# First-softmax maxima moved from one VectorE reduction to a ScalarE copy, GpSimd folds and a short VectorE minimum, with a new table of slots

## The chip, the core and the metric

The kernel runs on one core of a Trainium2 chip. The core has five engines that run their own instruction queues in order and wait for each other through semaphores: TensorE (PE; its weight loads are shown as PEld), VectorE (DVE), ScalarE (ACT), GpSimd (POOL) and SyncE (SP, which here only starts DMA transfers). SBUF is the on-chip memory of 128 partitions, PSUM the eight banks that PE writes. The metric is the device time of one execution in microseconds (us). Three runs of the kernel before took 719.73 to 719.92 us, median 719.89.

## The reference

```
def _attn_ref(x, inducing):            # x: 4 x 12416 x 128, inducing: 32 x 128
    scale = 1.0 / np.sqrt(C)
    I = np.broadcast_to(inducing[None], (B, m, C))
    def mab(q, kv):
        s = scale * (q @ kv.transpose(0, 2, 1))
        s = s - s.max(-1, keepdims=True)
        a = np.exp(s)
        a /= a.sum(-1, keepdims=True) + 1e-09
        return a @ kv
    h = mab(I, x)
    return mab(x, h)

def _moe_ref(x, w_gate, w_val, w_out): # x: 49664 x 128, d_ff 1536
    gate = 1.0 / (1.0 + np.exp(-(x @ w_gate)))
    val = x @ w_val
    return gate * val @ w_out
```

The 32 inducing rows attend over each batch's 12416 tokens (the first softmax, over tokens), each token then attends over the 32 results `h` (the second softmax, over 32), and a gated feed-forward layer follows.

## The kernel before

**Tiling.** A batch's 12416 tokens lie as 97 columns of 128 tokens, cut into six groups of 16 columns and a single column (group index 6). The feed-forward layer works on blocks of four columns (512 tokens): 24 blocks a batch and one last block made of the four single columns, 97 in all. The hidden width of 1536 is 12 chunks of 128. The weights are multiplied with `h` once a batch (`hw`), so that a chunk of a block needs a matmul with only 32 rows.

**Steps and slots.** Chunks are taken two and one at a time; a step has two chunks or one, a slot is a pair of steps, so three chunks. In a step `product` (L964) writes the value matmuls `v`, then the gate matmuls of two steps later (`gate_fill`), then DVE's product `u = (t + 1) * v` (L981), where `t = tanh(g/2)` comes from ACT (`gate`, L962). At the end of each odd step `project` (L1050) takes up to 12 or 16 output matmuls of 128 columns (L1062) from a queue; a finished block is scaled by ACT into `o` (L1081) and sent out by SP. A batch lasts 96 slots, and `base[b]` is its first.

**Work beside the steps.** Everything else is put into slots by hand. `at(slot, make, late)` keeps a list; `beside` calls what stands there: plain entries behind the even step of the slot, late ones behind the odd step, those with `side` inside `product`. An entry's instructions go to their engines' queues at that place.

- First softmax of batch b+1, during batch b (`plan_stage1`, L332): in slot `score` PE writes scores of one group into a PSUM bank (`s1_score_pe`, L255) and DVE takes the negated maximum over 512 columns (`s1_max`, L267); one slot later ACT takes the exponential with that maximum as bias (`s1_exp`, L280); in the next SP transposes the result by DMA (L304); later PE sums (`s1_sum_pe`) and ACT keeps the sums (L330). The groups have maxima of their own; `plan_combine` joins them.
- Second softmax (`plan_stage2`, L617): PE scores (L483), ACT copies to SBUF (`s2_take`, L520), POOL finds the maximum of 32 by five levels of subtract, clip at 0 and add (`s2_lower_pool`, L530 to L535), ACT takes the exponential (L544), POOL sums, inverts and spreads (L552 to L598), SP transposes into `a2r` (L609), from which the gate and value matmuls read.
- Asides (`plan_aside`, L1007): nine chunks of batch 3 are left out of the steps; ACT and POOL make their product instead of DVE.
- Loads of `x` for batch b+2 (b+1 in batch 0) are DMA transfers started by POOL (L96); SP transposes them into `xT` (L105).

**Banks.** PSUM has one bank each for `g1`, `v1`, `m` and `acc` and two each for `g2` and `v2`. All beside work takes turns on `m`.

Batch 0's own first softmax is in the prologue (`PROLOGUE`, the functions beginning with `p_`), ahead of the first product at 30.5 us.

Of the kernel before, what the change touches and what calls it, by code (L numbers as in the profile page):

```python
# [37 lines left out]
def kernel(  # L38
# [179 lines left out]

    summed = [0] * B
    def keep_on(n, tag):  # L220
# [11 lines left out]
    def at(slot, make, late=False, side=False):  # L232
        plan.setdefault((slot, "side" if side else late), []).append(make)
# [15 lines left out]
    def s1_score_pe(b, s, tag, s1=None):  # L249
        c0, n = groups[s]  # L250
        ng, w, R = s1_dims(s)
        if s1 is None:
            s1 = ps.tile([P, 512], F32, tag=tag, name="s1_ps")
# [35 lines left out]
    def s1_turn_pe(b, s, a1T, tag="m"):  # L289
        ng, w, R = s1_dims(s)  # L290
        aT = ps.tile([P, 4, P], F16, tag=tag, name="aT_ps")
# [15 lines left out]
    def s1_sum_pe(b, s, a1, hp, k0, k1):  # L307
        c0, n = groups[s]
# [23 lines left out]
    def plan_stage1(b, s, score, total):  # L332
# [15 lines left out]
        at(score, begin)  # L348
        at(score + 1, weigh, late=full)
        at(score + 2, turn)  # L350
        first, second, keep = total

        def part(k0, k1):
            if k0 == 0:
                st["hp"] = ps.tile([P, C + 1], F32, tag="m", name="hp_ps")
# [4 lines left out]
        at(keep, lambda: s1_sum_keep(b, s, st["hp"]))  # L360
# [21 lines left out]
    def hw_fill(b, hf, tag):  # L382
        hw_ps = ps.tile([P, NI // 2, P], F32, tag=tag, name="hw_ps")
# [32 lines left out]
    def plan_combine(b, lead, weights, fill):  # L416
# [36 lines left out]
        def total():  # L453
            lh = ps.tile([P, 2, m], F32, tag="m", name="lh_ps")
# [4 lines left out]
        def part(hf):  # L459
            st["hw_ps"] = hw_fill(b, hf, "m")  # L460

        def keep(hf):
            if hf == 0:
                st["hwt"] = bp.tile([P, NI, P], F16, tag="hw", bufs=B, name="hwt")
            nc.scalar.copy(out=st["hwt"][:, ts(hf, NI // 2), :], in_=st["hw_ps"][:])
            if hf == 1:
# [724 lines left out]
```

## Time and profile before

| | us |
|---|---|
| median of three runs | 719.89 |
| span of the profiled execution, first to last instruction | 718.4 |
| first product starts | 30.51 |
| last product ends | 714.0 |
| products on DVE (771) | 670.9 |
| tanh on ACT (770) | 589.5 |

The profiled execution's own time is its span plus what lies around it; the runs' median is 1.5 us above the span. In a row of groups stand line, engine, operation, what is written and read with its shape, the count, then the busy time in us and the mean of one instruction in ns, then the idle time of the engine just before them and what ended most of it. Rows of one engine can overlap by some tens of ns, since the next instruction begins before the last is written out; the busy time counts such a stretch once. In a timeline row stand start, duration, engine, line and count of merged neighbours. The queues have names with q (SPq, DVEq).

### The profile page before, as it was taken

The page shows a single profiled execution, that of the slowest core. Times are in us where ns is not written, and L with a number is a line of the kernel's source. Part 1 is how long each engine was busy: PE and PEld are TensorE (multiplying, and loading weights), DVE is VectorE, ACT ScalarE, POOL GpSimd, SP SyncE. Part 2 cuts the span into 40 slices and gives each one's busy share as a digit, 9 for nine tenths or more (in the row PEclk, how much of TensorE's full clock was granted, in tenths as well). Part 3 has the DMA queues.
Part 4 walks back from the last instruction along what each step waited for, and adds up shares of the span by engine and source line. Part 5 has one row for each costly group of instructions (what it writes and reads, how often), then busy time and mean ns, then how long its engine had stood idle before and what let it go on. Part 6 is the DMA issues. An engine that isn't in the chain of part 4 may idle for free.

```text
span 718.4 us, 21566 instructions
## 1 busy us (share of the span) xinstructions
PE 650.5 (91%) x8446; PEld 394.2 (55%) x8446; DVE 702.4 (98%) x872; ACT 675.1 (94%) x1019; POOL 445.8 (62%) x718
## 2 busy tenths in 40 slices
PE   8889889999998998999989988999899999999897
PEld 4455555555555555555555555555555555555555
DVE  5899999999999999999999999999999999999997
ACT  4699999999999999999999999999999999999996
POOL 4574763888653747588666266387766787676220
PEclk9999999999999999999999999999999999999999
DMA  9796696244568344335268431220222122223011
GB/s 209 115 182 130 125 165 105 75 90 106 89 133 162 80 103 92 59 79 119 66 117 161 102 75 51 70 74 31 77 60 73 46 62 67 39 75 71 35 46 46
DMA packets 118182, 65.77 MB, mean 92 GB/s; under 512 B 101408, under 2 KB 102208, under 8 KB 118080
## 3 DMA queue, kind: packets, MB, share of 16 engines
q1 hardware_dynamic: 112176, 50.90, 31.6%
q0 software_dynamic: 5584, 13.34, 10.9%
q8 instruction: 66, 1.08, 0.6%
q14 instruction: 36, 0.29, 0.1%
q10 hardware_dynamic: 320, 0.15, 0.1%
HBM read 27.80 MB, written 25.43 MB: 74 GB/s over the span
## 4 chain that ended last, share of the span: by engine, by line
PE 51%; ACT 24%; DVE 16%; issue 5%; DMA 2%; DVEq 1%; POOL 1%; ACTq 0%
PE acc_ps L1062 24%; ACT t L962 22%; PE v_ps L944 21%; DVE u L981 14%; PE g_ps L944 2%; DMA xn<-in_x_dram 2%; PE s_ps L483 2%; PE hp_ps L315 1%; ACT o L1081 1%; DVE nm L267 1%; DVEq L981 1%; ACT a1T L280 0%; PE s_ps L255 0%; POOL xn L96 0%; ACTq L962 0%
## 5 line engine op out<-in xcount | busy, mean ns | idle before, releaser
L981 DVE SCALAR_TENSOR_TENSOR u<-t,v_ps 128x1024 f16<-128x1024 f16 (+1 forms) x771 | 670.9, 945 | 1.7 <-PE g_ps L944 0.8
L962 ACT ACTIVATE t<-g_ps 128x1024 f16<-128x1024 f32 (+1 forms) x770 | 589.5, 822 | 22.2 <-ACT t L962 10.3
L944 PE MATMUL v_ps<-a2r,hwt 32*128 32x512 f16 (+1 forms) x1179 | 290.8, 371 | 56.9 <-DVE u L981 53.2
L1062 PE MATMUL acc_ps<-wo,u 128*128 128x128 f16 x4620 | 324.5, 220 | 0.9
L1062 PEld LDWEIGHTS <-u 128*128 128x128 f16 x4620 | 259.9, 98 | 89.5 <-issue 88.1
L944 PE MATMUL g_ps<-a2r,hwt 32*128 32x512 f16 (+1 forms) x1179 | 294.0, 376 | 0.0
L944 PEld LDWEIGHTS <-hwt 32*128 32x128 f16 x2382 | 93.5, 91 | 188.6 <-issue 142.2
L552 POOL TENSOR_TENSOR sum<-e 128x256 f32<-128x256 f16 (+1 forms) x23 | 15.5, 672 | 133.8 <-ACT e L544 130.0
L598 POOL TENSOR_TENSOR a2n<-e,rs 128x2048 f16<-128x2048 f16 (+3 forms) x25 | 86.8, 3474 | 4.8 <-DVE rs L570 3.1
L576 POOL TENSOR_TENSOR near<-sme,minus 128x16 f32<-128x16 f32 (+1 forms) x22 | 65.3, 2966 | 1.8
L1081 ACT ACTIVATE o<-acc_ps 128x512 f32<-128x512 f32 x96 | 58.4, 609 | 0.0
L531 POOL TENSOR_SCALAR rise<-rise 128x256 f32<-128x256 f32 (+6 forms) x110 | 51.2, 466 | 9.7
L532 POOL TENSOR_TENSOR top<-top,rise 128x128 f32<-128x128 f32 (+3 forms) x88 | 28.4, 323 | 7.3
L552 POOL TENSOR_TENSOR sum<-sum 128x128 f32<-128x128 f32 (+3 forms) x92 | 28.4, 309 | 7.2
L530 POOL TENSOR_TENSOR rise<-top 128x128 f32<-128x128 f32 (+3 forms) x88 | 27.3, 310 | 6.9
L530 POOL TENSOR_TENSOR rise<-sc 128x256 f32<-128x256 f32 (+1 forms) x22 | 16.3, 739 | 20.9 <-ACT sc L520 20.6
L1031 POOL TENSOR_TENSOR xn_spare<-xn_spare 128x512 f16<-128x512 f32 x9 | 11.4, 1270 | 22.2 <-ACT xn_spare L1029 22.0
L535 POOL TENSOR_TENSOR sc<-sc,top 128x512 f32<-128x512 f32 (+1 forms) x22 | 23.9, 1086 | 1.7
L1026 POOL TENSOR_SCALAR xn_spare<-xn_spare 128x512 f32<-128x512 f16 x9 | 13.4, 1493 | 11.2 <-ACT xn_spare L1025 11.2
L483 PEld LDWEIGHTS <-xT 128*128 128x128 f16 x388 | 13.1, 96 | 11.7 <-issue 11.3
L280 ACT ACTIVATE a1T<-s_ps,nm 128x512 f16<-128x512 f32 (+1 forms) x26 | 16.4, 630 | 3.1 <-DVE nm L267 3.0
L483 PE MATMUL s_ps<-hT,xT 128*128 128x32 f16 x388 | 18.1, 178 | 0.1
(150 smaller groups left out, 291.4 us busy)
## 6 DMA issues: line engine op xcount, KB each, us to landing
out_dram<-o SPq DMA_DIRECT2D x96, 256.0 KB, 2.2
xn<-in_x_dram POOLq DMA_DIRECT2D x18, 512.0 KB, 7.7
xn<-in_x_dram POOLq DMA_DIRECT2D x3, 544.0 KB, 6.9
xn<-in_x_dram POOLq DMA_DIRECT2D x3, 256.0 KB, 12.8
xn<-in_x_dram SPq DMA_DIRECT2D x1, 576.0 KB, 4.8
xn<-in_x_dram SPq DMA_DIRECT2D x1, 512.0 KB, 3.9
a2r<-a2n SPq DMA_TRANSPOSE x29, 4.5
wg<-in_moe_w_gate_dram POOLq DMA_DIRECT2D x1, 384.0 KB, 12.7
```

What stands on the lines that cost most here:

```text
L483: nc.tensor.matmul(s2[:, j, :], xT[b][:, c + j, :], hT16[b][:], start=(j == 0), stop=whole and j == j1 - 1, skip_group_check=True,)
L530: nc.gpsimd.tensor_tensor(out=r, in0=far, in1=near, op=ALU.subtract)
L531: nc.gpsimd.tensor_scalar_max(out=r, in0=r, scalar1=0.0)
L532: nc.gpsimd.tensor_tensor(out=top[:, 0:n, 0:w], in0=near, in1=r, op=ALU.add)
L552: nc.gpsimd.tensor_tensor(out=d[:, 0:n, :], in0=src[:, :, 0:w], in1=src[:, :, w : 2 * w], op=ALU.add)
L576: nc.gpsimd.tensor_tensor(out=near[:, 0:n], in0=sme[:, 0:n], in1=minus1[:, 0:n], op=ALU.pow)
L598: eng.tensor_tensor(out=a2n[:, 0:n, :, :], in0=e.unsqueeze(2).to_broadcast((P, n, 4, m)), in1=rs.unsqueeze(2).unsqueeze(3).to_broadcast((P ...
L944: st[what + "end"] = nc.tensor.matmul(pt[:, k, col : col + nb * P], hw[b][r : r + 32, j // 2, :], a2r[r : r + 32, o : o + nb, :].rearrange ...
L962: st["tanh"] = nc.scalar.activation(out=st["t"][:], in_=st["g"][:], func=AF.Tanh, scale=0.5)
L981: u = nc.vector.scalar_tensor_tensor(out=st["u"][:, :, c:e], in0=st["t"][:, :, c:e], scalar=1.0, in1=st["v"][:, :, c:e], op0=ALU.add, op1= ...
L1062: nc.tensor.matmul(acc[0][(i // 2) % len(acc[0])][:, i, :], u[:, ts(i, P)], wo16[:, j, :], start=(i in fresh), stop=not any(e[2] == ib and ...
L1081: nc.scalar.mul(out=o32[:], in_=acc[0][0][:], mul=0.5)
```

## The change

Some first-softmax groups of batches 1 to 3 get another way to their maximum. In slot `score` PE writes the scores and ACT copies them, negated, to SBUF (`leave`). POOL folds the 512 columns to 64 by three levels of subtract, clip and subtract (`lower_tree`). In a later slot `done` DVE takes the minimum of the 64 (`finish`), and in slot `weight` or behind it ACT takes the exponential from the SBUF copy (`weigh_low`). A group with six slots in the table goes this way, one with four as before. The slots of nearly all beside work come from a new table, `TIMES`: its first entry serves batch 0, the second batches 1 and 2, the third batch 3. In the second some groups are scored in slots below zero, that is in the batch before, and the `xT` transposes (`turn`) stand nine slots ahead of their scores. The slots of the `x` loads are the same.

Besides: the asides leave out the last chunks of a block, and steps may hold chunks of two blocks; some aside fills and takes have another place in the step; projections of a block may run early or finish a block when 28 (in two blocks 20) or more matmuls wait; pools of `u`, `t` and `o` shrink. `BEHIND`, `DROPPED` and `SWAP` are empty and `GAP` is 0, so that the code that reads them changes nothing.

```diff
-ASIDE = {3: ((2, 9, 3, 8), (11, 17, 7, 1), (23, 26, 7, 0), (50, 53, 15, 3), (58, 62, 19, 11), (64, 69, 19, 10), (73, 76, 20, 5), (78, 81, 23, 11), (83, 88, 23, 10))}
-LATE = (4, 19, 32, 46, 43)
+ASIDE = {3: ((-1, 'm', 7, 'm', 3), (11, 'm', 17, 'm', 7), (23, 'mf', 27, 'm', 7), (50, 'm', 53, 'm', 14), (58, 'mf', 62, 'm', 19), (66, 'm', 69, 'm', 19), (73, 'm', 76, 'm', 19), (80, 'ma', 81, 'm', 23), (84, 'm', 92, 'ma', 23))}
+BEHIND = ()
+DROPPED = ()
+SWAP = ()
+GAP = 0
+BRISK = (81, 93)
+TIMES = (
+    {
+        "late": {2: (6, 7, 13, None), 3: (18, 19, 27, None), 4: (31, 33, 45, None), 5: (56, 57, 65, 52)},
+        "sum": ((10, 19, 22, 35, 35, 35), (13, 40, 41, 41), (25, 33, 37, 48, 49, 50), (37, 51, 51, 51), (42, 48, 49, 55, 55, 55), (45, 54, 54, 54), (22, 27, 27, 30)),
+        "join": (57, 61, (76, 78), (81, 83)),
+        "next": ((73, 74, 81), (86, 87, 94)),
+        "turn": (3, 7, 16, 21, 31, 37, 12),
+    },
+    {
+        "late": {2: (0, 3, 18, None), 3: (16, 21, 34, None), 4: (36, 37, 50, None), 5: (56, 57, 65, 52)},
+        "sum": ((9, 17, 17, 34, 35, 35), (13, 18, 26, 47, 48, 49), (-6, 3, 6, 50, 51, 51), (29, 35, 39, 45, 46, 46), (-3, 23, 24, 25), (31, 42, 42, 54, 55, 55), (39, 42, 43, 43)),
+        "join": (56, 60, (76, 78), (81, 83)),
+        "next": ((72, 74, 81), (86, 87, 93)),
+        "turn": (0, 4, -15, 20, -12, 22, 30),
+    },
+    {
+        "late": {2: (4, 6, 14, None), 3: (19, 21, 29, None), 4: (32, 34, 42, None), 5: (46, 48, 56, 43)},
+    },
+)
+LOW = 64
+NEGS = 4
...
-    up = ctx.enter_context(tc.tile_pool(name="up", bufs=6))
-    tp = ctx.enter_context(tc.tile_pool(name="tp", bufs=4))
-    op = ctx.enter_context(tc.tile_pool(name="op", bufs=4))
+    up = ctx.enter_context(tc.tile_pool(name="up", bufs=4))
+    tp = ctx.enter_context(tc.tile_pool(name="tp", bufs=3))
+    op = ctx.enter_context(tc.tile_pool(name="op", bufs=3))
+    sp = ctx.enter_context(tc.tile_pool(name="sp", bufs=1))
...
+    def lower_tree(low, neg):
+        w, src = 2 * P, neg
+        rise1 = s2p.tile([P, (GC + NLO) * (m // 2)], F32, tag="sum16", name="rise1")
+        top1 = s2p.tile([P, (GC + NLO) * (m // 2)], F32, tag="sum16", name="top1")
+        while w >= LOW:
+            near, far = src[:, 0:w], src[:, w : 2 * w]
+            r = rise1[:, 0:w]
+            nc.gpsimd.tensor_tensor(out=r, in0=near, in1=far, op=ALU.subtract)
+            nc.gpsimd.tensor_scalar_max(out=r, in0=r, scalar1=0.0)
+            dst = low if w == LOW else top1
+            nc.gpsimd.tensor_tensor(out=dst[:, 0:w], in0=near, in1=r, op=ALU.subtract)
+            src = dst
+            w //= 2
...
+        def leave():
+            st["neg"] = sp.tile([P, 4 * P], F32, tag="neg", name="neg", bufs=NEGS)
+            st["low"] = sp.tile([P, LOW], F32, tag="low1", name="low1", bufs=NEGS)
+            nc.scalar.mul(out=st["neg"][:], in_=st["s1"][:], mul=-1.0)
+            side_done()
+            lower_tree(st["low"], st["neg"])
+
+        def finish():
+            nm, _, col = s1_col(b, s)
+            nc.vector.tensor_reduce(
+                out=nm[:, col], in_=st["low"][:], axis=AX.X, op=ALU.min
+            )
+
+        def weigh_low():
+            nm, _, col = s1_col(b, s)
+            st["a1T"] = s1p.tile([P, 512], F16, tag="a1T", name="a1T")
+            nc.scalar.activation(
+                out=st["a1T"][:], in_=st["neg"][:], func=AF.Exp, bias=nm[:, col], scale=-1.0
+            )
+
+        if len(total) > 3:
+            done, weight, *total = total
+            at(score, fill)
+            at(score, leave, late=True)
+            at(done, finish)
+            at(weight, weigh_low, late=True)
+            at(weight + 1, turn)
+        else:
+            at(score, begin)
+            at(score + 1, weigh, late=full)
+            at(score + 2, turn)
...
     for i, n in enumerate(apart):
+        odd = (chunks[-1][1] + 1) % 2 if chunks else 0
+        js = [*range(odd, NJ), *range(odd)]
+        chunks += [(i, j) for j in js[: NJ - n]]
+        beyond.append(js[NJ - n :])
...
-            ready = waiting(t - 1)
+            room = 3 * BC - early if behind or not brisk else 3 * BC
             if acc[0] is None:
-                pace = 4 * BC if ready >= 6 * BC else 3 * BC
-            project(t - 1, t, pace)
+                brisk = waiting(t - 1) >= (5 if queue and queue[-1][2] in quick else 7) * BC
+                if brisk:
+                    room = 4 * BC
+            elif block_left() <= 4 * BC - early:
+                room = block_left()
+            project(t - 1, t, room)
```

More of the change, by code (lines that the diff above doesn't have):

```diff
@@ L217, with side_tile, side_done, side_swap @@
         )
+    side = {"acc": "acc", "m": "m", "used": 0}
+    def side_tile(shape, dtype, name):
+        side["used"] += 1
+        return ps.tile(shape, dtype, tag=side["m"], name=name)
+    def side_done():
+        side["used"] -= 1
+    def side_swap(slot):
+        if side["used"] == 0 and slot in SWAP:
+            side["acc"], side["m"] = side["m"], side["acc"]
     summed = [0] * B
+    tensor_uses = [0]
     def keep_on(n, tag):
@@ L230, with at @@
     plan = {}
-    def at(slot, make, late=False, side=False):
-        plan.setdefault((slot, "side" if side else late), []).append(make)
+    def at(slot, make, late=False):
+        slot -= sum(d <= slot for d in DROPPED)
+        plan.setdefault((slot, late), []).append(make)
     def s1_col(b, s):
@@ L968, in product @@
             keep_on(3, "acc")
-        gate_fill(t + 2)
+        if t % 2 == 0:
+            beside(t // 2, "first")
+        if t // 2 not in behind_at:
+            gate_fill(t + 2)
+            if t % 2 == 0:
+                beside(t // 2, "next")
+        elif t % 2:
+            gate_fill(t + 1)
+            gate_fill(t + 2)
         if t % 2:
@@ L1015, in fill @@
             nc.tensor.matmul(
-                st[what][:],
+                st[what][:, 0, :],
                 hw[b][r : r + 32, j // 2, :],
@@ L1084, in project @@
                 acc[0] = None
+                side_swap(now // 2)
                 if now < NST:
                     return
-    base = [first_step[(b, 0)] // 2 for b in range(B)]
     for b in range(B):
@@ L1140, in waiting, with block_left @@
         return n
-    for a in aside:
-        plan_aside(*a)
+    def block_left():
+        return sum(1 for e in queue if e[2] == queue[-1][2])
+    for b, table in ASIDE.items():
+        for n, (g, gb, v, vb, i) in enumerate(table):
+            k = sum(e[-1] == i for e in table[:n])
+            i += b * NG * GC // BC
+            plan_aside(base[b] + g, gb, base[b] + v, vb, i, beyond[i][k])
     for t in range(2):
```

178 lines of the change are left out of this document (103 added, 75 removed).

## The prediction

> **What bounds the kernel now.** I read the page first: busy times, then the costliest groups.
>
> ```profile
> span 718.4 us, 21566 instructions
> PE 650.5 (91%) x8446; PEld 394.2 (55%) x8446; DVE 702.4 (98%) x872; ACT 675.1 (94%) x1019; POOL 445.8 (62%) x718
> ...
> L981 DVE SCALAR_TENSOR_TENSOR u<-t,v_ps 128x1024 f16<-128x1024 f16 (+1 forms) x771 | 670.9, 945 | 1.7 <-PE g_ps L944 0.8 <-PE v_ps L944 0.2
> ```
>
> DVE is busy for 98% of the span, and in front of its 771 products it stood idle for 1.7 us in all. The chain of waits names PE and ACT more often, but only as the way a product's inputs came; the idle column decides. Next the four batches, from the first product to the last, by busy time:
>
> ```profile
> core 0: us, PE busy (x) PEld busy (x) DVE busy (x) ACT busy (x) POOL busy (x), PEclk, DMA share, GB/s
> 30.51:202.14 171.63, 155.31 (x2065) 94.25 (x2065) 171.35 (x207) 165.25 (x247) 114.24 (x191) 1.00 0.64 121
> 202.14:372.72 170.58, 155.25 (x2057) 94.35 (x2057) 170.54 (x205) 164.51 (x247) 110.55 (x184) 1.00 0.48 99
> 372.72:543.17 170.45, 154.84 (x2057) 94.14 (x2057) 170.45 (x204) 164.50 (x247) 107.11 (x178) 1.00 0.32 78
> 543.17:714.00 170.83, 159.33 (x1941) 97.34 (x1940) 169.46 (x196) 164.99 (x245) 100.38 (x135) 1.00 0.21 56
> ```
>
> DVE fills every batch to within 0.3 us, except the last with its tail. So whatever leaves DVE shortens the kernel, as long as nobody else comes late. The slack beside it: about 6 us a batch on ACT, 15 on PE, 57 to 70 on POOL. A slot (two steps, three chunks) lasts about 1.73 us.
>
> **Maxima on DVE: the gain.** The forms of DVE's reductions, and one in its place:
>
> ```profile
> L267 DVE TENSOR_REDUCE nm<-s_ps 128x1 f32<-128x512 f32 x22 | 15.0, 683 | 0.1
> ...
> L267 DVE TENSOR_REDUCE nm<-s_ps 32x1 f32<-32x128 f32 x4 | 1.1, 271 | 0.0
> ...
> L424 DVE TENSOR_REDUCE ml<-nm 128x1 f32<-128x7 f32 x3 | 0.5, 153 | 0.0
> ```
> ```profile
> 217.10 0.68 DVE L267 TENSOR_REDUCE nm<-s_ps 128x1 f32<-128x512 f32 x1
> 217.70 5.27 DVE L981 SCALAR_TENSOR_TENSOR u<-t,v_ps 128x512 f16<-128x512 f16 x6
> ```
>
> The 683 ns of a row overlap the next instruction by about 80 ns (217.10 to 217.70 is 0.60 us). The overlap is the same before and after, so I take differences of rows. A minimum over 64 does not occur. Between 7 elements at 153 ns and 512 at 683 ns lies 1.05 ns an element, so 64 cost 153 + 57 x 1.05 = 213 ns, and a group saves 683 - 213 = 470 ns. Bounds: 153 ns (530 saved) and the 128-element row, 271 ns (412 saved). The description says 12 groups; in the table I count those with six slots: 3 in the first entry and 5 in the second, which serves two batches, so 13. Gain: 13 x 0.470 = **6.1 us**, bounds 5.4 and 6.9; with 12 groups 5.6.
>
> [...]
>
> **ACT: copies added, hidden.**
>
> ```profile
> 209.11 1.51 ACT L962 ACTIVATE t<-g_ps 128x1024 f16<-128x1024 f32 x2 [0.22 <-ACT t L962]
> 210.51 0.60 ACT L1081 ACTIVATE o<-acc_ps 128x512 f32<-128x512 f32 x1
> 210.99 3.10 ACT L962 ACTIVATE t<-g_ps 128x1024 f16<-128x1024 f32 x4
> ```
> ```profile
> L520 ACT COPY sc<-s_ps 128x512 f32<-128x512 f32 x22 | 13.1, 595 | 0.0
> L544 ACT ACTIVATE e<-sc 128x512 f16<-128x512 f32 x18 | 11.4, 635 | 0.0
> ...
> L516 ACT ACTIVATE e<-s_ps 128x512 f16<-128x512 f32 x1 | 0.6, 603 | 0.0
> ```
>
> A scaled copy of this size holds ACT for 0.48 us (210.51 to 210.99). The exponential now reads SBUF: 635 against 603 ns, 0.03 more. A new group thus adds 0.51 us; five in a batch add 2.6 while the batch shrinks by 2.35. ACT's idle 6.1 us becomes about 1.1, in batch 0 (three groups) 3.4. That covers it only as an average. A plain slot leaves ACT 0.22 us or more, so one copy is worked off in about two slots; the table sets copies on slots other than those with a block's `o`. Cost taken: 0. Without this cover 13 x 0.51 = 6.6 us would return. The copy frees PSUM bank `m` in its own slot instead of one slot later, so no later fill waits longer for it.
>
> **POOL: folds added; who stands behind them.**
>
> ```profile
> 46.91 0.73 POOL L530 TENSOR_TENSOR rise<-sc 128x256 f32<-128x256 f32 x1
> ...
> 52.43 0.24 POOL L530 TENSOR_TENSOR rise<-top 128x32 f32<-128x32 f32 x1
> ...
> 54.46 1.08 POOL L535 TENSOR_TENSOR sc<-sc,top 128x512 f32<-128x512 f32 x1
> ```
> ```profile
> 200.84 0.67 POOL L552 TENSOR_TENSOR sum<-e 128x256 f32<-128x256 f16 x1 [5.25 <-ACT e L544]
> ...
> 207.41 3.61 POOL L598 TENSOR_TENSOR a2n<-e,rs 128x2048 f16<-128x2048 f16 x1
> ```
>
> The second softmax's fold chain takes 46.91 to 55.54 = 8.63 us; its first three levels have the shapes of the new folds: 46.91 to 52.43 = **5.52 us** a group. Its sums, inverse and spread take 200.84 to 211.02 = 10.18 us. In batches 1 and 2 five groups add 27.6 us to 107 to 111, inside 168.
>
> What matters is the queue. Behind each fold stand sums, spreads and `x` loads; behind the minimum on DVE stands every later product, and behind that PE's fills. The tightest minimum is slot 18 of batches 1 and 2. From slot 88.2 of the batch before (its chain's copy is done) the queue holds chain 8.63, folds 5.52, sums and spread 10.18, chain 8.63, folds 5.52 twice: 44.0 us or 25.3 slots, so ready at 17.5; DVE gets there at 18.65. Margin 2.0 us, cost 0. Each microsecond beyond it would be one on DVE.
>
> Does a busier POOL slow DVE? Two stretches of 8 us, POOL busy for 6.75 and for 0.00 us:
>
> ```profile
> 47.00:55.00 8.00, 6.89 (x86) 3.93 (x82) 8.00 (x11) 7.66 (x13) 6.75 (x16) 1.00 1.07 211
> 57.00:65.00 8.00, 7.25 (x101) 4.54 (x101) 8.00 (x10) 7.64 (x12) 0.00 (x0) 1.00 1.08 179
> ```
> ```profile
> L981 DVE SCALAR_TENSOR_TENSOR u<-t,v_ps 128x1024 f16<-128x1024 f16 x5 | 6.1, 1211 | 0.0
> ```
> ```profile
> L981 DVE SCALAR_TENSOR_TENSOR u<-t,v_ps 128x1024 f16<-128x1024 f16 x5 | 6.1, 1213 | 0.0
> ```
>
> 1211 and 1213 ns: no.
>
> **Second-softmax slots moved.** Every group still does the same work; its exponential stands on ACT in an earlier slot, and waits there for the chain on POOL, with the gates of later steps behind it. The tightest are slots 13 and 27 of batch 0.
>
> ```profile
> 58.08 0.68 ACT L280 ACTIVATE a1T<-s_ps,nm 128x512 f16<-128x512 f32 x1
> ```
>
> At the end of slot 14 ACT began this exponential at 58.08; one slot earlier, and without the 0.60 of group 0's reduction in slot 9, is 55.75. The chain is done at 55.54: 0.2 us to spare. Slot 27 lies 14 slots on, with some 0.4 of short reductions: 55.75 + 14 x 1.73 + 0.4 = 80.4. The chain, by the sum in the paragraph on loads, ends at 80.5: about even, and a tenth is within the 0.22 us that ACT idles in a plain slot. Cost 0, up to 0.5. The transposes into `a2r` follow the spread on SP and land 4.5 us later:
>
> ```profile
> a2r<-a2n SPq DMA_TRANSPOSE x29, 4.5
> ```
>
> Group 3 of batch 1 has the least: spread done at slot 42.9, landed at 45.5, first gate in slot 47. Cost 0.
>
> **Loads and transposes behind POOL: the loss I expect.** From batch 1 on, transposes stand nine slots (15.6 us) ahead of their scores. Batch 0 keeps its slots, but its loads are issued by POOL, which now gets to them later.
>
> ```profile
> 84.78 1.71 POOL L96 DMA_DIRECT2D xn<-in_x_dram  x3
> ```
> ```profile
> DMA to landing us min/median/max: 5.1/7.9/15.1
> ```
> ```profile
> 90.13 7.41 SPq L105 DMA_TRANSPOSE xT<-xn  x1
> ```
> ```profile
> L105 SPq DMA_TRANSPOSE xT<-xn x21: 1142/1871/7411, 35.5 to 404.1; - x21
> ...
> DMA to landing us min/median/max: 2.4/4.4/11.5
> ```
> ```profile
> 111.05 0.40 PE L255 MATMUL s_ps<-xT,indT 128*32 128x512 f16 x4
> ```
>
> Before, three loads left POOL at 84.78, the last two those of group 5 of batch 1 and group 0 of batch 2. Now the queue from 46.91 holds chain, folds, sums and spread, load, chain (to 80.5), load, folds, sums and spread: 8.63 + 5.52 + 10.18 + 0.65 + 8.63 + 0.65 + 5.52 + 10.18 = 50.0, so group 5's load leaves at 96.9. It lands 5.1 to 7.9 us later (the two landing rows are those of the loads and of the `xT` transposes), at 102.0 to 104.8. Its transpose, next on SP, lands 4.4 to 11.5 us after its issue; a load under way, here group 0's, holds it up, as in the 7.41 us row. So `xT` is there between 106.4 and 116.3, middle 111.4. PE wants it in slot 45: before, slot 44's score ran at 111.05. One slot (1.73) later, with two groups' 0.47 and one reduction of 0.60 (group 4's, not yet due) saved by then, is 111.2. PE is in order, so the products' fills wait behind that score: 0 to 5.1 us. The middle gives 0.2; a third load (group 1 of batch 2) leaves POOL one chain later, at about 106.8, while the transpose may be under way, so I take more: **0.8**.
>
> **Tail and the rest.** The aside table keeps nine entries, all in batch 3. Counting the projection queue through its rules leaves 24 matmuls instead of 16 behind the last step and takes 12 instead of 16 in it: 36 in a row instead of 32.
>
> ```profile
> 712.28 2.00 PE L1062 MATMUL acc_ps<-wo,u 128*128 128x128 f16 x32
> ```
>
> At 62 ns each, +0.25 us. Smaller pools for `u`, `t`, `o` and chunk pairs across blocks: 0, since ACT and DVE run at most two steps apart and projections lag about one slot.
>
> **Sum.** -6.1 + 0.8 + 0.25 = -5.05; the profiled 718.4 becomes 713.35. The runs' median is 719.89, 1.5 above the profiled span for what lies around it: **714.8 us**.
>
> **Rivals.**
> (a) The transpose for slot 45 comes late in full: 5.1 us instead of 0.8 gives 719.1, no change; 3 us gives 717. For it: 7.41 us on SP behind loads. Against: the middle of the bounds is near the deadline.
> (b) Slower: the minima wait for POOL. Place: `finish`, on DVE. It decides once folds are over 2.0 us later than laid out; at 1 us a group it returns 13 and gives 714.8 + 13 = 728; break-even is 0.4 a group. For it: POOL's 62% rises to some 72%, all in order. Against: the durations are of a DVE already 98% busy.
> [...]
> (d) The change moves 12 groups: 715.3.
>
> **Chances.** Forecast with its bounds, 713.0 (6.9 saved, no wait, no longer tail) to 716.8 (5.4 saved, 2.1 us of waits, the tail): 0.68, (d) in it. Part of (a) or crowded ACT, 716.8 to 718.4: 0.15. (a) in full: 0.08. (b) 0.08, (c) 0.01. Under 0.2% (1.4 us) this kernel's measurement can't tell from no change: faster 0.83, same 0.08, slower 0.09. Range 713.0 to 718.6.
>
> **What would show it.** Right: 5 reductions of 512 left in batches 1 to 3 (18 before) beside 13 short ones near 213 ns, DVE down 6 us, its idle before products up by 1 us or less, at slot 45 of batch 0 (about 110 us in), released by PE. Wrong: idle ahead of the short reductions released by POOL (b); ACT waiting on nothing while DVE waits for `t` (no cover on ACT); products longer than 1213 ns (c).

## The result: slower by half a per cent, and where the time went

The changed kernel takes 722.62 us (median of six executions, 721.6 to 725.3) against 719.90 before: a ratio of 1.0046, 95% interval 1.0036 to 1.0055. The forecast was 714.8, its range ended at 718.6. The profiled execution, 725.3 us long with a span of 723.4, is the longest of the six; one cost below is larger in it than in the others, and the text says so there.

Four rows of the changed kernel's profile page (in this kernel the products have line L1096, the gate and value fills L1051, the projections L1194):

```profile
span 723.4 us, 21727 instructions
PE 663.9 (92%) x8446; PEld 399.3 (55%) x8446; DVE 699.4 (97%) x872; ACT 678.0 (94%) x1032; POOL 506.3 (70%) x835
...
PEclk9999998999999999999999999999999999999999
...
L1096 DVE SCALAR_TENSOR_TENSOR u<-t,v_ps 128x1024 f16<-128x1024 f16 (+1 forms) x771 | 674.0, 946 | 4.5 <-PE g_ps L1051 2.4
```

DVE's busy time fell by 3.0 us (702.4 to 699.4) while the span grew by 5.0: DVE waits more than it saves. An 8 stands in the clock row, which had only 9s before, in the slice from 108.5 to 126.6 us. By stage, again from the first product to the last, with busy times in the order PE, PEld, DVE, ACT, POOL, then the granted clock:

```profile
core 0: us, PE busy (x) PEld busy (x) DVE busy (x) ACT busy (x) POOL busy (x), PEclk, DMA share, GB/s
29.61:208.99 179.38, 159.51 (x2073) 96.49 (x2072) 171.54 (x207) 166.47 (x252) 131.87 (x224) 0.98 0.63 118
208.99:378.87 169.88, 159.44 (x2064) 96.09 (x2063) 169.22 (x205) 165.92 (x252) 133.91 (x229) 1.00 0.47 100
378.87:547.93 169.06, 159.25 (x2050) 95.79 (x2048) 168.47 (x203) 164.99 (x250) 127.91 (x220) 1.00 0.32 75
547.93:718.73 170.80, 160.06 (x1932) 96.59 (x1932) 169.69 (x196) 164.82 (x244) 99.16 (x131) 1.00 0.20 56
```

Against the rows of before, batch 0 is 7.75 us longer, batches 1 and 2 are 0.70 and 1.39 shorter, and batch 3 is unchanged. (The first product comes 0.9 us earlier; kernels with the same prologue start it between 29.5 and 30.5 here.) The reductions on DVE and the new instructions on ACT, by form:

```profile
L309 DVE TENSOR_REDUCE nm<-s_ps 128x1 f32<-128x512 f32 x9 | 6.1, 686 | 5.9 <-PE s_ps L297 5.7
L420 DVE TENSOR_REDUCE nm<-low 128x1 f32<-128x64 f32 x13 | 2.8, 212 | 0.0
```
```profile
L427 ACT ACTIVATE a1T<-neg,nm 128x512 f16<-128x512 f32 x13 | 9.5, 733 | 0.0
L414 ACT ACTIVATE neg<-s_ps 128x512 f32<-128x512 f32 x13 | 8.1, 626 | 0.0
```

So 13 groups went the new way, a short minimum takes 212 ns, and DVE lost 13 x (683 - 212) = 6.1 us of work, as forecast. Its busy time fell by 3.0 only, because that counts an overlap of two rows once and the products' rows overlap less now: their busy time rose from 670.9 to 674.0 us while the mean of one rose by 1 ns (945 to 946). None of the 13 minima waited for POOL (the last column is 0.0). One of the nine long reductions waited 5.7 us for PE.

By batch: batch 0 has three new groups, and by slot -3 each batch does one long reduction of 0.6 for the next, so that batch 0 has one more and batch 2 one less. That makes 3 x 0.471 - 0.6 = 0.8 less in batch 0, 5 x 0.471 = 2.4 less in batch 1 and 2.4 + 0.6 = 3.0 less in batch 2. Batches 1 and 2 came down by 0.70 and 1.39 only, so 1.7 and 1.6 us of new waits stand in them. In batch 0 7.75 + 0.8 = 8.55 us were added.

**Slot 45 of batch 0.** POOL's and SP's transfers of the changed kernel around it (start, duration of the issue), then the chain of waits:

```profile
95.60 1.18 POOL L122 DMA_DIRECT2D xn<-in_x_dram  x2
105.36 0.61 POOL L122 DMA_DIRECT2D xn<-in_x_dram  x1
```
```profile
95.69 6.97 SPq L713 DMA_TRANSPOSE a2r<-a2n  x1
...
103.36 4.67 SPq L131 DMA_TRANSPOSE xT<-xn  x1
```
```profile
103.36 13.68 DMA xT<-xn
117.04 0.04 issue
117.08 0.62 PE s_ps L297 x4
```

Group 5's load and that of batch 2's group 0 leave POOL at 95.60. The transpose into `xT` goes out at 103.36. While SP is still issuing it (4.67 us), the third load leaves at 105.36; the transpose lands 13.68 us after its issue, at 117.04, and the score that needs it runs then. The timeline of DVE and three stretches by busy time show the price:

```profile
103.85 8.16 DVE L1096 SCALAR_TENSOR_TENSOR u<-t,v_ps 128x1024 f16<-128x1024 f16 x9
117.75 0.69 DVE L309 TENSOR_REDUCE nm<-s_ps 128x1 f32<-128x512 f32 x1 [5.75 <-PE s_ps L297]
118.36 0.68 DVE L1096 SCALAR_TENSOR_TENSOR u<-t,v_ps 128x512 f16<-128x512 f16 x1
120.21 3.10 DVE L1096 SCALAR_TENSOR_TENSOR u<-t,v_ps 128x1024 f16<-128x1024 f16 x3 [1.18 <-PE g_ps L1051]
```
```profile
107.30:114.50 7.20, 3.10 (x36) 1.93 (x36) 4.70 (x6) 4.67 (x7) 4.72 (x9) 1.00 1.23 157
114.50:121.30 6.80, 4.22 (x32) 2.31 (x32) 2.38 (x3) 2.11 (x4) 1.50 (x4) 0.50 0.77 122
121.30:128.50 7.20, 6.78 (x111) 4.35 (x108) 7.14 (x10) 7.11 (x12) 6.62 (x8) 1.00 0.19 57
```
```profile
L1051 PE MATMUL g_ps<-a2r,hwt 32*128 32x512 f16 x6 | 1.5, 383 | 0.0
```
```profile
L1051 PE MATMUL v_ps<-a2r,hwt 32*128 32x512 f16 x4 | 1.6, 610 | 0.0
L297 PE MATMUL s_ps<-xT,indT 128*32 128x512 f16 x4 | 0.6, 602 | 6.4 <-DMA xT<-xn 6.4
```

The last three rows are PE's, the first of them from 107.3 to 114.4, the others from 114.5 to 121.3. DVE stands still for 5.75 us. PE is idle for 6.4 us. From 114.5 to 121.3 its granted clock is 0.50 (1.00 in the stretches on both sides), the first fills after the wait take 610 ns instead of 383, and DVE loses another 1.18 us. Counted from each product's start to the next start, the place costs 7.1 us in this execution. The rest of batch 0's 8.55, and the 3.3 of batches 1 and 2, are mostly waits of 0.1 to 0.3 us, some eight in a batch.

### The profile page after: what moved, and what is told of

Read it like the earlier page. It is cut to its first block, busy times and chain, and to the rows that moved or that the text cites. A ratio compares the mean times of both kernels' runs of the same rounds, so it can differ in the third digit from the quotient of the medians.

```text
span 723.4 us, 21727 instructions
## 1 busy us (share of the span) xinstructions
PE 663.9 (92%) x8446; PEld 399.3 (55%) x8446; DVE 699.4 (97%) x872; ACT 678.0 (94%) x1032; POOL 506.3 (70%) x835
## 4 chain that ended last, share of the span: by engine, by line
PE 53%; ACT 22%; DVE 15%; issue 5%; DMA 3%; POOL 1%; DVEq 1%; ACTq 0%; SPq 0%; POOLq 0%
PE acc_ps L1194 25%; PE v_ps L1051 21%; ACT t L1069 19%; DVE u L1096 14%; PE g_ps L1051 3%; DMA xT<-xn 2%; PE s_ps L587 2%; DMA xn<-in_x_dram 1%; ACT o L1213 1%; PE hp_ps L359 1%; PE s_ps L297 1%; DVEq L1096 1%; ACT a1T L427 0%; ACT sc L624 0%; PE xt_ps L816 0%
## 5 line engine op out<-in xcount | busy, mean ns | idle before, releaser
L1096 DVE SCALAR_TENSOR_TENSOR u<-t,v_ps 128x1024 f16<-128x1024 f16 (+1 forms) x771 | 674.0, 946 | 4.5 <-PE g_ps L1051 2.4
L1051 PE MATMUL v_ps<-a2r,hwt 32*128 32x512 f16 (+1 forms) x1179 | 291.3, 373 | 41.8 <-DVE u L1096 34.8
L1194 PE MATMUL acc_ps<-wo,u 128*128 128x128 f16 x4620 | 325.7, 220 | 1.6
L1194 PEld LDWEIGHTS <-u 128*128 128x128 f16 x4620 | 261.9, 98 | 95.4 <-issue 93.6
L1051 PE MATMUL g_ps<-a2r,hwt 32*128 32x512 f16 (+1 forms) x1179 | 293.8, 376 | 0.0
L1051 PEld LDWEIGHTS <-hwt 32*128 32x128 f16 x2382 | 96.7, 91 | 176.1 <-issue 125.1
L384 POOL TENSOR_SCALAR rise<-rise 128x256 f32<-128x256 f32 (+2 forms) x39 | 22.5, 577 | 3.4
```

The lines of the kernel that those rows point to most:

```text
L1051: st[what + "end"] = nc.tensor.matmul(pt[:, k, col : col + nb * P], hw[b][r : r + 32, j // 2, :], a2r[r : r + 32, o : o + nb, :].rearrange ...
L1096: u = nc.vector.scalar_tensor_tensor(out=st["u"][:, :, c:e], in0=st["t"][:, :, c:e], scalar=1.0, in1=st["v"][:, :, c:e], op0=ALU.add, op1= ...
L1194: nc.tensor.matmul(acc[0][(i // 2) % len(acc[0])][:, i, :], u[:, ts(i, P)], wo16[:, j, :], start=(i in fresh), stop=not any(e[2] == ib and ...
```

## The experiments

Every time is a median with its ratio to the kernel before on the same chip; that kernel took 719.7 to 719.9 in all of them. Diffs are against the changed kernel unless another is named. "Small waits" are those in batches 0 to 2 outside slot 45, summed from each product's start to the next start, less the other DVE work between them, over the usual 1.131 us (0.598 for one chunk): 0.96 us before, 5.7 in the changed kernel.

### The late transpose

**e1**, the third load ten slots later:

```diff
-when = ((24, 33, 42, 60, 60, 82) if b else (33, 37, 60, 60, 78, 82))[g]
+when = ((24, 33, 42, 60, 60, 82) if b else (33, 47, 60, 60, 78, 82))[g]
```

> The changed kernel with one load moved: group 1 of batch 2 from slot 37 to slot 47 of batch 0, so that it leaves POOL about 10 us behind the transpose of group 5 instead of 2 us. Theory H (a load under way holds the transpose up, here above all the one started behind it): the transpose lands 5 to 8 us after its issue at 103.4 instead of 13.7, PE's wait in slot 45 goes from 6.4 us to under 1, and the clock keeps its full grant; time 722.6 - 4 to 7 = 715.6 to 718.6. Theory L (group 5's own load, landing at 102.8, is too late whatever follows): the wait stays above 4 us and the time within 1 us of 722.6.

718.54 us, ratio 0.9979 (0.9969 to 0.9990): 4.1 us come back from moving one load by ten slots.

**e2**, group 5's load seven slots earlier, the third load left where it was:

```diff
-at(o + (None, 4, 5, 17, 24, 31)[g], lambda g=g: x_load(1, g))
+at(o + (None, 4, 5, 17, 24, 24)[g], lambda g=g: x_load(1, g))
```

> The changed kernel with the load of group 5 of batch 1 moved from slot 31 to slot 24 of batch 0, so that it leaves POOL at about 80 instead of 95.6; the two loads of batch 2 stay. Theory L: no wait in slot 45, time 715.6 to 718.6. Theory H: the transpose still stands on SP behind one into a2r and beside a load of batch 2; it is issued about 2 us earlier, before the load at 105.4, and lands before the score at about 111 if that is enough; a wait of 0 to 3 us is left, time 716 to 720.

718.42 us, ratio 0.9982 (0.9973 to 0.9992). The `xT` tiles between 95 and 120 us in the two kernels, the first in e1, the second in e2 (who waits, and from issue to landing):

```profile
  DMA xT<-xn: 0.5, 1
...
DMA to landing us min/median/max: 8.2/8.2/8.2
```
```profile
DMA to landing us min/median/max: 5.0/5.0/5.0
```

The transpose goes out at nearly the same time in both (103.22 and 103.74) and lands after 8.2 and 5.0 us instead of 13.68. In e2 the third load still leaves 2.2 us behind the transpose (105.91) and does no harm: with one load less under way SP has issued the transpose in 2.34 us, by 106.08, and it has landed at 108.7. So the price is that of two loads meeting one transpose, an earlier one still landing when it was issued and a later one leaving POOL 2.0 us behind its issue; to take away either was enough (PE waits 0.5 us for `xT` in e1, not at all in e2, 6.4 us in the changed kernel).

The packets of the changed kernel show how a load holds a transpose up. Below are packets, MB and share of the 16 engines by queue (q1 is SP's queue, q0 POOL's) from 98 to 100 us, when two loads land beside the transpose into `a2r`, then from 108 to 109 and from 109 to 117 us:

```profile
q0 software_dynamic: 91, 0.37, 92.7%
q1 hardware_dynamic: 92, 0.02, 8.9%
```
```profile
q1 hardware_dynamic: 1134, 0.29, 127.6%
```
```profile
q1 hardware_dynamic: 1123, 0.27, 65.8%
q0 software_dynamic: 144, 0.52, 57.7%
```

In the 2 us beside the two loads the queues move packet for packet, 91 and 92, but the loads' packets have 4096 bytes and the transposes' 256. With no load SP's queue moves 1134 packets in one microsecond; once the third load's packets come in, from 109.0 us on, it moves 1123 in eight. The transpose and the third load landed together, at 117.0 and 117.2.

**e3**, the kernel before with its loads as late as the change made them:

```diff
-at(o + (None, 4, 5, 17, 24, 31)[g], lambda g=g: x_load(1, g))
+at(o + (None, 4, 5, 17, 24, 36)[g], lambda g=g: x_load(1, g))
-when = ((24, 33, 42, 60, 60, 82) if b else (33, 37, 60, 60, 78, 82))[g]
+when = ((24, 33, 42, 60, 60, 82) if b else (36, 37, 60, 60, 78, 82))[g]
```

> The kernel before with nothing changed but two load slots in batch 0: group 5 of batch 1 from slot 31 to 36 and group 0 of batch 2 from 33 to 36, so that both leave POOL at about 98 instead of 86. Theories H and L: PE waits for xT at the score in slot 44 (about 111) for 3 to 8 us, the granted clock drops for some us behind it, time 719.9 + 3 to 8 = 723 to 728, with every maximum still on VectorE as before. If the stall of the changed kernel comes from its folds, copies or minima and not from the loads' lateness: 719.9 within 0.5.

720.16 us, ratio 1.0025 (1.0002 to 1.0049). Seven of ten executions took 719.2 to 720.9, three 724.1 to 727.1 with a mean granted clock of 0.991 to 0.995. In the profiled one, of the seven, the transpose landed in time, 6.9 us after its issue. Of the 99 executions on record of the kernel before as it stands, only two went above 721 us (723.1 and 724.0, with clocks of 0.989 and 0.994). So the lateness alone seems to bring the stall into the kernel before too, but only now and then, like a race between transfers whose price varies. That the three long executions stalled at slot 44 is inferred from their clock (the changed kernel's profiled execution, with its stall, has 0.994; the other seven here have 0.999 to 1.000); none of them was profiled.

### Whose time the new way saves

**e6**, against e1: the 13 maxima are taken by DVE over 512 again, in the score's slot; ACT's copies and the new table stay.

```diff
-st["s1"] = s1_score_pe(b, s, "m")
+st["s1"] = s1_score(b, s, "m")
...
-lower_tree(st["low"], st["neg"])
...
-nc.vector.tensor_reduce(out=nm[:, col], in_=st["low"][:], axis=AX.X, op=ALU.min)
+pass
```

> As the run with the third load moved, but the 13 groups' maxima are taken by VectorE over 512 columns in the score's slot as before; the ScalarE copy, its exponential from SBUF and the whole new table stay, the folds and the short minima go. Theory G (VectorE's time is the only price): slower than the third-load run by 13 x 0.47 = 6.1 us. Theory S (the 0.60 us pause of the products in a score's slot used to give PE time for its scores, and without it products wait 0.1 to 0.3 us in slots with work beside them): the small waits, 5.6 us in batches 0 to 2 of the changed kernel against 1.0 before, shrink to 1 to 3, and it is slower by 2.5 to 5 us only.

724.89 us, ratio 1.0072 (1.0057 to 1.0087): 6.35 above e1, against 6.1 of DVE time. The small waits stay at 5.2 us in all. The idea that DVE's long reductions had been pauses in which the other engines caught up, so that giving them back would end the waits, falls as a whole. One part of it stands: the waits in and behind the slots where a new group is scored (10, 11, 31, 90) are gone when a reduction stands there, and others appear (19, 20, 44).

### Code or table

**e8**, the old slots in the new code (the two most telling entries of the second table; the first table and the other entries go back too):

```diff
-"late": {2: (0, 3, 18, None), 3: (16, 21, 34, None), 4: (36, 37, 50, None), 5: (56, 57, 65, 52)},
+"late": {2: (4, 6, 18, None), 3: (20, 22, 34, None), 4: (36, 38, 50, None), 5: (56, 58, 66, 52)},
-"sum": ((9, 17, 17, 34, 35, 35), (13, 18, 26, 47, 48, 49), (-6, 3, 6, 50, 51, 51), (29, 35, 39, 45, 46, 46), (-3, 23, 24, 25), (31, 42, 42, 54, 55, 55), (39, 42, 43, 43)),
+"sum": ((8, 15, 16, 17), (12, 18, 19, 19), (24, 31, 31, 31), (28, 35, 35, 35), (40, 47, 48, 49), (44, 50, 51, 51), (32, 43, 43, 43)),
```

> The changed kernel's code with the slots of the kernel before written into its table: no group goes the new way, all 18 maxima stay 512 wide on DVE; the smaller pools, the chunk pairs, the projection pace and the new asides stay. Theory T (the small waits of 4.6 us in batches 0 to 2 come from where the new table puts ACT's and PE's beside work): the small waits fall to about 1 us and the time is that of the kernel before plus the longer tail, 719.9 + 0.3 = 720.2, within 0.7. Theory C (they come from the code: the smaller pools of u, t and o, or the projections that run early): the 5 us of small waits stay, and the time is 720.2 + 4.6 = 724.8, within 1.

720.48 us, ratio 1.0010 (1.0001 to 1.0019). Small waits 2.1 us, 0.98 of them in a single place. The code is nearly free; the waits come with the table, that is with its slots and with the 13 groups that it puts on the new way. This run does not part these two.

**e4**, against e1:

```diff
-up = ctx.enter_context(tc.tile_pool(name="up", bufs=4))
+up = ctx.enter_context(tc.tile_pool(name="up", bufs=6))
-NEGS = 4
+NEGS = 2
```

> The changed kernel with the third load in slot 47 (718.5), and with the u pool at 6 again instead of 4, two tiles for the negated copies instead of 4. Theory C, if it is the u pool: most of the 4.6 us of small waits go, 714 to 715. Theory T: no difference, 718.5 within 0.7.

718.48 us, ratio 0.9983 (0.9974 to 0.9992), with the same waits in the same slots as e1: not the pool of `u`. Those of `t` and `o` are as small in e8, where the waits are few.

**e5**, against e1, the pace of projections in batches 0 to 2:

```diff
...
+if tensor_uses[0] != slot_used and owed == 0 and block_left() > 4 * BC:
+    room, owed = 2 * BC, BC
+elif tensor_uses[0] == slot_used and owed:
+    room, owed = room + owed, 0
```

> The changed kernel with the third load in slot 47 (718.5), in batches 0 to 2 with 8 projections instead of 12 in a slot in which PE has beside work, and the four left over done in the next slot that has none. If PE's load in a slot makes the fills late (beside work and projections together), the small waits shrink by half or more: 715.5 to 716.5. If ACT's copies and exponentials are late by themselves, no difference: 718.5 within 0.7.

723.37 us, ratio 1.0050 (1.0037 to 1.0064), worse by 4.8 than e1, so the forecast was a miss. But no other run's slots tell as much. In batch 1 e1 waits in slots 0, 11, 23, 31, 41, 86 and 90 (0.13 to 0.27 us each). In e5 slots 23, 31, 41, 86 and 90 take 8 projections instead of 12, and of these five only slot 23 still waits (0.18). Instead 17 of the 18 slots that take 16 projections, without any beside work, wait 0.12 to 0.29 us, and the small waits double to 10.5 us. So it is PE's load in the slot that makes such a wait, and PE has nowhere to put it: four matmuls, 0.25 us, are more than a plain slot has to spare. The 15 us a batch that PE idled before are 0.16 us in each of 96 slots.

### Where the table's entries stand

**e7**, against e8: four of the seven groups of batches 1 and 2 the new way, in the old slots.

```diff
-"sum": ((8, 15, 16, 17), (12, 18, 19, 19), (24, 31, 31, 31), (28, 35, 35, 35), (40, 47, 48, 49), (44, 50, 51, 51), (32, 43, 43, 43)),
+"sum": ((8, 16, 16, 23, 23, 23), (12, 19, 19, 26, 26, 26), (24, 33, 33, 39, 39, 39), (28, 37, 37, 42, 42, 42), (40, 47, 48, 49), (44, 50, 51, 51), (32, 43, 43, 43)),
```

> The kernel of the old table, with four of the seven groups of batches 1 and 2 (scores in slots 8, 12, 24 and 28) put on the new way to their maximum; everything else stands where it stood. 8 groups x 0.47 = 3.8 us less on DVE. Theory T: 720.2 - 3.8 = 716.4, if the added copies find ACT idle; if each new group costs waits as it did in the changed kernel (4.6 us for 13 groups, 0.35 each), 716.4 + 2.8 = 719.2. Theory C: 724.8 - 3.8 = 721.0.

725.02 us, ratio 1.0074 (1.0061 to 1.0087): slower than the changed kernel with all of its 13. Batches 1 and 2 are 346.06 us long, against 341.03 before, with 3.8 less work: 8.8 us of new waits from eight groups.

**e10**, against e7:

```diff
-"sum": ((8, 16, 16, 23, 23, 23), (12, 19, 19, 26, 26, 26), (24, 33, 33, 39, 39, 39), (28, 37, 37, 42, 42, 42), (40, 47, 48, 49), (44, 50, 51, 51), (32, 43, 43, 43)),
+"sum": ((9, 17, 17, 23, 23, 23), (13, 21, 21, 26, 26, 26), (25, 33, 33, 39, 39, 39), (29, 37, 37, 42, 42, 42), (40, 47, 48, 49), (44, 50, 51, 51), (32, 43, 43, 43)),
```

> The kernel of the old table with four new groups (725.0), with the scores, and so ACT's copies, one slot later (9, 13, 25, 29 instead of 8, 12, 24, 28) and the first two exponentials in slots 17 and 21 instead of 16 and 19; the sums stay, all four parts of a group in one slot. Theory N (a copy or exponential that stands in ACT's queue straight ahead of a block's o makes the tanh behind both late by about 0.33 us; elsewhere it is hidden): the waits of 0.30 to 0.35 us in slots 9, 13, 17, 21, 25 and 29 of both batches go, 12 x 0.32 = 3.9, 721.1. Theory W (ACT simply has no more room, wherever the copies stand): the waits move to other slots, 725.0 within 1.

723.45 us, ratio 1.0054 (1.0041 to 1.0067). The same stretch of ACT in slots 8 and 9 of batch 1, first in e7, then in e10, each with DVE's row behind it:

```profile
217.36 0.60 ACT L414 ACTIVATE neg<-s_ps 128x512 f32<-128x512 f32 x1
217.83 0.62 ACT L1213 ACTIVATE o<-acc_ps 128x512 f32<-128x512 f32 x1
218.31 4.71 ACT L1069 ACTIVATE t<-g_ps 128x1024 f16<-128x1024 f32 x6
```
```profile
219.69 3.55 DVE L1096 SCALAR_TENSOR_TENSOR u<-t,v_ps 128x1024 f16<-128x1024 f16 x4 [0.23 <-PE v_ps L1051]
```
```profile
217.09 0.61 ACT L1213 ACTIVATE o<-acc_ps 128x512 f32<-128x512 f32 x1
217.57 1.53 ACT L1069 ACTIVATE t<-g_ps 128x1024 f16<-128x1024 f32 x2
218.95 0.65 ACT L414 ACTIVATE neg<-s_ps 128x512 f32<-128x512 f32 x1
```
```profile
213.91 9.88 DVE L1096 SCALAR_TENSOR_TENSOR u<-t,v_ps 128x1024 f16<-128x1024 f16 x11
```

Where the copy stands right ahead of the block's `o`, ACT is away from tanh for 0.95 us and DVE waits; one slot later, with two tanh between them, DVE runs through eleven products. The waits of slots 9, 13, 17, 25 and 29 are gone in both batches. But other waits grew, so that only 1.85 of the expected 3.9 us came back in these two batches (346.06 to 344.21). PE's waits in this kernel say which (the first row stands in e7 as well, the second is new), with one of them in place:

```profile
PE hp_ps L359 <- ACT sc L624: 2.3, 4, 0.6
PE hp_ps L359 <- ACT neg L414: 1.2, 2, 0.6
```
```profile
248.89 0.24 PE L359 MATMUL hp_ps<-xn,a 128*32 128x128 f16 x4 [0.59 <-ACT neg L414]
```

All beside work shares bank `m`. A sum whose slot follows that of a copy out of `m` stands at the head of PE's queue until ACT has emptied the bank, and the products' fills stand behind it. The copies of slot 25 are now nearer to the sums of slot 26, and the wait there went from 0.26 to 0.79 us.

**e9**, against e10:

```diff
-"sum": ((9, 17, 17, 23, 23, 23), (13, 21, 21, 26, 26, 26), (25, 33, 33, 39, 39, 39), (29, 37, 37, 42, 42, 42), (40, 47, 48, 49), (44, 50, 51, 51), (32, 43, 43, 43)),
+"sum": ((9, 17, 17, 23, 24, 24), (13, 21, 21, 30, 31, 31), (25, 35, 37, 42, 43, 43), (28, 35, 35, 35), (40, 47, 48, 49), (44, 50, 51, 51), (32, 46, 46, 46)),
```

> The kernel of the old table with three new groups in batches 1 and 2 (6 in all, 2.8 us less on DVE), their copies off the slots ahead of an o as in the run beside it, and their sums parted over two slots instead of one. Theory N, with PE's part (32 to 36 of PE's beside matmuls in one slot cost 0.26 to 0.90 us, half of them little): 720.5 - 2.8 and some 0.5 left, 718.2 within 0.8. Theory W: each new group costs waits as in the kernel with four of them, (725.0 + 3.8 - 720.5) / 8 = 1.04 against 0.47 saved, 720.5 + 6 x 0.57 = 723.9.

721.48 us, ratio 1.0026 (1.0016 to 1.0036), about half way between the two theories. To part the sums helped little, because the first half stood behind a copy or exponential out of `m` again (slots 22 and 41, waits of 0.73 and 0.39 us in slots 23 and 42).

**e11**, against e2, the table for batches 1 and 2:

```diff
-"sum": ((9, 17, 17, 34, 35, 35), (13, 18, 26, 47, 48, 49), (-6, 3, 6, 50, 51, 51), (29, 35, 39, 45, 46, 46), (-3, 23, 24, 25), (31, 42, 42, 54, 55, 55), (39, 42, 43, 43)),
+"sum": ((9, 17, 17, 34, 35, 35), (13, 18, 23, 47, 48, 49), (-6, 3, 6, 50, 51, 51), (27, 35, 39, 45, 46, 46), (-3, 25, 26, 26), (30, 42, 42, 54, 55, 55), (39, 42, 43, 43)),
```

> The changed kernel with group 5's load in slot 24 (718.4), and in its table for batches 1 and 2 four places moved: the sums of the group scored in slot -3 from 23 and 24 to 25 and 26 (bank m is by then free of the copy of slot 21), the copies of slots 29 and 31 to 27 and 30, one exponential from 26 to 23. Theory N (a sum straight behind ACT's copy from bank m, and two copies close ahead of an o, each cost 0.25 to 0.28 us): the waits of slots 23 and 31 go in both batches, 4 x 0.26 = 1.05 us, 717.4. Theory W (ACT has no more room wherever they stand): they come up in other slots, 718.4.

718.52 us, ratio 0.9985 (0.9976 to 0.9994), no better than e2. The waits of slots 23 and 31 (0.25 and 0.28) became waits in 23, 25, 26 and 30 (0.15, 0.26, 0.09 and 0.17). In this full table the waits that were mended came up next door.

### How much is ACT's, how much PE's

**e12**, against e2, the copies cut to 64 columns (the other 448 of each tile are set to zero once, at the start):

```diff
-nc.scalar.mul(out=st["neg"][:], in_=st["s1"][:], mul=-1.0)
+nc.scalar.mul(out=st["neg"][:, 0:64], in_=st["s1"][:, 0:64], mul=-1.0)
...
```

> The changed kernel with group 5's load in slot 24 (718.4), in which ACT's 13 negated copies take 64 columns instead of 512; the other 448 columns of the four copy tiles are set to zero once ahead of the first block, so the maxima and weights of those groups are not the reference's. Folds, minima, exponentials, sums, slots and DVE's work stay. Theory W (ACT has no room left in slots 0 to 55, so what is added to it comes out as late tanh and late fills): 13 x some 0.4 us less on ACT there, the 5.5 us of small waits in batches 0 to 2 fall below 2.5, 715 to 716. If ACT's load is not what makes them (PE's packed sums, the bank m, POOL): 718.4 within 0.7.

717.19 us, ratio 0.9966 (0.9952 to 0.9979). The copies take 250 ns instead of 623, 4.8 us less in all, and the waits of slots 11 and 31 are gone, but those of 23, 41, 86 and 90 stay. The small waits fall by 1.3 us, from 5.5 to 4.2: ACT's room is a part, and less of it than expected.

**e13**, against e2, the sums cut to a quarter:

```diff
+few = 1 if b else w
-for k in range(k0, min(k1, w)):
+for k in range(k0, min(k1, few)):
...
-stop=(k == w - 1),
+stop=(k == few - 1),
```

> The changed kernel with group 5's load in slot 24 (718.4), in which PE sums only a quarter of each group's columns in the first softmax of batches 1 to 3 (8 matmuls a group instead of 32), so that those sums are not the reference's; ACT's copies stay 512 wide. Theory P (besides ACT, PE has no room in the slots in which the new table packs the sums: 23, 51, 52, 54, 55): the waits there go, about 1.1 us in batches 0 to 2, 717.3; those of slots 11, 31, 86 and 90 stay. If the sums do not matter: 5.5 us of waits stay, 718.4.

717.60 us, ratio 0.9964 (0.9946 to 0.9982). The small waits fall by 0.74 us where 1.1 was expected: those in slots 35, 54 and 55 of batch 0 end, those of 23 and 51 shrink.

**e14**, both edits:

> Both: ACT's copies of 64 columns (717.2 alone) and a quarter of the sums; maxima, weights and sums of those groups are not the reference's. Theory W and P together: 5.5 - 1.3 - 1.1 = 3.1 us of small waits left in batches 0 to 2, 716.1. If both only move one and the same shortage about: 717.2 again.

716.58 us, ratio 0.9960 (0.9946 to 0.9975). Batches 0 to 2 together, by the sum row of the stretches, with e2's full work, with short copies, and with both:

```profile
sum 511.08, PE 476.77 PEld 287.54 DVE 508.94 ACT 497.21 POOL 394.65; mean PE 158.92 PEld 95.85 DVE 169.65 ACT 165.74 POOL 131.55
```
```profile
sum 509.79, PE 474.49 PEld 286.83 DVE 508.20 ACT 493.25 POOL 396.41; mean PE 158.16 PEld 95.61 DVE 169.40 ACT 164.42 POOL 132.14
```
```profile
sum 509.12, PE 470.69 PEld 282.89 DVE 507.97 ACT 493.28 POOL 395.46; mean PE 156.90 PEld 94.30 DVE 169.32 ACT 164.43 POOL 131.82
```

511.08 to 509.12 is 1.96 us; the two parts alone gave 1.29 and 0.74. They very nearly add, so they are two shortages, not one. About 3.5 us of small waits are left against 0.96 before. By e5 at least three of those in batch 1 are PE's too: the waits of slots 41, 86 and 90 stay with short copies and go with fewer projections, while that of slot 31 goes with either. Slots 10 and 90 wait where PE writes a new group's scores with no reduction on DVE in the slot, and e6, with the reduction, has no wait there. How the rest divides over PE's scores and transposes was not tried one by one.

## Why the prediction was wrong

In the profiled execution the account is: 6.1 us saved, 7.1 lost in slot 45, 4.7 more in small waits (5.7 - 0.96), 0.3 in the tail, 0.9 gained ahead of the first product: +5.1, measured +5.0.

- **The gain** was right to a tenth: 13 groups, 212 ns for a minimum forecast at 213, 6.1 us; e6 gave 6.35 when it was undone.
- **The term for slot 45** was mis-sized and is the larger error. The place, the releaser and the queue on POOL were right (group 5's load forecast for 96.9, out at 95.60; the third for 106.8, out at 105.36). The step that failed was the choice of 0.8 between 0 and 5.1, and the upper bound itself: it took the longest landing seen, 11.5 us, of a transpose whose loads had all left POOL before it was issued (the row of 7.41 us), and it left out the granted clock (1.18 of the 7.1 us). The third load was named there and priced at 0.6; it cost nearly everything. Measured: 7.1 in the longest execution, 4.1 and 4.2 by the medians of e1 and e2.
- **ACT at cost 0** failed. The text itself said that the idle time covered the copies "only as an average", and then used the average. Short copies give back 1.3 us of the changed kernel's small waits; right ahead of an `o` a copy cost 0.3 (e7). Slots 8 to 15 and 24 to 31 of batch 1, before and then in e1, show what the average hid (length, then the busy times; PE is the first and ACT the fourth):

```profile
216.30:230.45 14.15, 12.02 (x160) 7.25 (x158) 14.15 (x18) 13.43 (x20) 5.79 (x15) 1.00 0.77 164
...
244.60:258.80 14.20, 12.09 (x173) 6.93 (x170) 14.20 (x18) 13.44 (x20) 10.65 (x19) 1.00 0.52 107
```
```profile
216.20:230.40 14.20, 13.84 (x164) 7.85 (x161) 14.15 (x18) 13.88 (x22) 11.27 (x24) 1.00 0.19 59
...
244.60:258.80 14.20, 13.54 (x170) 7.88 (x169) 14.01 (x18) 14.02 (x22) 12.53 (x23) 1.00 0.55 114
```

ACT had 0.72 and 0.76 us to spare there and has 0.32 and 0.18; PE went from 2.1 to 0.4 and 0.7. By the code neither can work ahead, since each fill waits for a bank that the product or the tanh of two steps before must leave.
- **The beside work that was moved, at cost 0** (bounds 0 to 0.5), failed too: with PE's sums cut to a quarter 0.74 us comes back (e13), and the prediction looked neither at PE's room in a single slot nor at who holds bank `m` when a sum begins. It did say that a copy frees the bank "in its own slot", which is true of the order in the code, not of the moment.
- **POOL** was right: the minima never waited, the products of two chunks take 1215 ns beside a POOL busy for 70% (1214 beside 62% before), so (b) did not happen, nor the longer products that (c) stands for, and (d) neither, with 13 groups. **The tail** came to 0.3 behind the last product (0.25 forecast), with 36 projections in a row, 2.18 us against 2.00:

```profile
717.24 2.18 PE L1194 MATMUL acc_ps<-wo,u 128*128 128x128 f16 x36
```

- **The rivals.** (a), the transpose late in full, was the right mechanism at too small a price, 719.1. What no rival held was (a) and crowded engines together; the range was built as if they shut each other out. With the load moved (e1, e2) the time is 718.4 to 718.5, at the edge of the range.

The best version of those that compute everything, the change with group 5's load in slot 24, takes 718.42 us, 0.2% below the kernel before: 1.3 us of the 6.1, by the kernel before on the same chip (719.75).

## What to carry to other kernels

When the busiest engine is at 98% and the next two at 91 to 94%, as here, where ACT's 6 us a batch were 0.72 us in the eight slots from slot 8, cover must be sought slot by slot: how long the other engine idles in the very stretch, what stands directly ahead and behind in its queue, and which shared bank the next user waits for. A transfer's landing time read from a place where no later transfer came in is not a bound once the change moves one beside it (here 11.5 us before, 13.68 after); give such a deadline more margin (here 6.4 us, nearly four slots, were missing), or move the other transfer, which here took one number. And where two costs can strike in one run, the range must hold their sum.

## What the hardware showed

- In the changed kernel PE stood idle for 6.4 us, from 110.7 to 117.1. At 114.5, 3.8 us into it, the granted clock fell from 1.00 to 0.50 and stayed there for 6.8 us, to 121.3, which is 4.2 us behind the first matmul at 117.1; fills took 610 ns instead of 383, and the wait's price rose by a fifth (1.18 us on 5.75).
- A DMA transpose of the same tile, issued at 103.7, 103.2 and 103.4 us, landed after 5.0 (e2), 8.2 (e1) and 13.7 us (the changed kernel), by which loads were beside it. Beside two loads, packets of 256 bytes and of 4096 went one for one from 98 to 100 us (92 and 91), where the transposes alone had 1134 in the 1 us from 108.
- Four matmuls of 62 ns more in a plain slot of 1.73 us made DVE wait 0.12 us or more in 17 of 18 slots (e5), though PE is idle for 8% of the time (0.14 us of such a slot).
